# One load instead of two for the first x chunk, and the last matmul pieces shared out differently, in a fused attention + token-mixing MLP kernel

## Chip, cores, metric

The kernel runs on one core of one Trainium2 chip. The metric is the device time of one execution in microseconds (us). Most numbers come from profiled executions. "PE" is the matmul engine (TensorE), "PEld" its weight loads, DVE, ACT and POOL are VectorE, ScalarE and GpSimd, SP is the queue that issues nearly all DMAs. Times inside a profile are counted from the start of its span; the device time is about 1.8 us longer than the span. A load is "issued" while its queue is busy starting it, and "lands" when the data has arrived.

## The reference, cut to what matters

```python
xn = layernorm(A_x)                     # 2048 tokens x 1024, 16 chunks of 128 tokens
out = A_x + attention(xn) + mlp(xn)

def attention(x):   # 32 heads of 32; 4 segments of 512 tokens, causal softmax inside a segment,
    ...             # plus a linear memory carried from segment to segment; then @ wo
def mlp(x):         # mixes tokens: u = gelu(h^T w1 + b1), y = u w2 + b2, with h = layernorm(x)
    ...             # w1 is 2048 x 3584, w2 is 3584 x 2048
```

## The kernel before: the parts that matter

The first hidden layer of the MLP needs normalised x, so the kernel begins with loads of x and w1, statistics on DVE (even chunks) and ACT (odd chunks), a power on POOL, and the scaling to `h` on DVE. Ten matmuls on zeros run meanwhile ("warm-up").

```python
# start: chunk 0 in two halves of 64 rows, one on SP's queue, one on ACT's
for h, issuer in enumerate(("sp", "act")):
    fw.dma(self.xin[64 * h:64 * h + 64, 0, :], self.x_d[64 * h:64 * h + 64, 0, :],
           writes=[(self.R_xin[0], self.R_xin0)[h]], issuer=issuer)
...
for kind, c0, n in (("x", 1, 1), ("x", 2, 1), ("w", 0, 2), ("x", 3, 1), ("x", 4, 2), ...):   # all on SP
...
for _ in range(self.N_WARM):                          # N_WARM = 10
    fw.mm(self.bank(0), self.warm[:, 0:P], self.warm[:], start=True, stop=True)
...
# DVE's order: D0 = statistics of chunk 0, d2 = half the statistics of chunk 2, h0 = scale chunk 0
NORM_ORDER = (["D0 A1 S0 d2 h0 A1' A3 S1 d2' h1"] + ...)
```

In the second half of the kernel the attention of 32 units (a unit is 4 heads of one segment) is interleaved on PE with "pieces": single 128x512 matmuls of the second MLP layer and of the output projection. The pieces fill the time in which PE would wait for exponentials, masks and copies of the attention.

```python
for u in range(N_UNIT):                     # 32 units
    n0, n1, n2 = self.share(u)
    self.logits(u, 0); self.main_emit(n0)   # n0 pieces
    if u and not last_of_seg(u - 1): self.combine(u - 1)      # DVE
    self.logits(u, 1); ...; self.main_emit(n1)
    self.weigh(u, 0); self.weigh(u, 1)      # PE; DVE copies each result out of PSUM
    self.proj_q(un, 0) if un < N_UNIT else self.main_emit(8)
    self.weigh(u, 2); ...; self.weigh(u, 3)
    if un < N_UNIT: self.proj_k(un, 1)
    if last_of_seg(u): self.combine(u)
    self.main_emit(n2)                      # n2 pieces behind the last weighing
self.tail()

def share(u):
    if u < N_UNIT - 4:
        return (11, 14, 7) if u < N_GRP else (11, 15, 8)
    return (11, 16, 10) if u < N_UNIT - 2 else (11, 16, 4) if u < N_UNIT - 1 else (11, 13, 7)

def tail(self):         # output projection of the last segment, added to rows stored earlier
    ... 4 reloads of those rows ("fin") on SP ...
    product(0, 0, 7); product(1, 0, 7)      # 14 matmuls that don't need unit 31
    self.o_transpose(u, 6)                  # 4 transposes of unit 31's result, after combine(31)
    product(2, 0, 7); ...                   # the rest; each product: DVE addition, store
```

A piece of which the last matmul is done leaves PSUM by an "eviction" on DVE (`scalar_tensor_tensor` into `stg`), and the finished chunk is stored by SP.

The softmax here doesn't subtract the row's maximum and nothing guards it: scores larger than these inputs give would overflow.

Of the kernel before, what the change touches and what calls it, by code (L numbers as in the profile page):

```python
# [29 lines left out]
N_UNIT = N_SEG * N_GRP  # L30
# [315 lines left out]
class _Kernel:  # L346
# [31 lines left out]
    def alloc(self):  # L378
        nc = self.nc
        a = self.keep = _Arena(nc, self.SB_BASE, self.SB_END)  # L380
        self.ident = a.take("ident", [P, P], BF16)
        self.brow1 = a.take("brow1", [P, 32], BF16)
        self.brow2 = a.take("brow2", [P, 32], BF16)
        self.bcol = a.take("bcol", [P, 2, 32], BF16)
        self.b1c = a.take("b1c", [P, N_FCH], F32)
        self.b2c = a.take("b2c", [P, N_TCH], F32)
        self.beta_sb = a.take("beta_sb", [P, N_HEAD], BF16)
        self.gcol = a.take("gcol", [P, N_HEAD], F32)
        self.gate = a.take("gate", [P, N_GRP, 2, 4], F32)
        self.eps8 = a.take("eps8", [P, 2, 4], F32)  # L390
        self.diag = a.take("diag", [P, 4, VW], F32)
        self.ln_st = a.take("ln_st", [P, N_TCH, 12], F32)
        self.ln_mv = a.take("ln_mv", [P, N_TCH, 2], F32)
        self.ln_rs = a.take("ln_rs", [P, N_TCH, 2], F32)
        self.expo = a.take("expo", [P, N_TCH], F32)
        self.ln_sm = a.take("ln_sm", [P, N_TCH, 1], F32)
        self.vA = [a.take(f"vA{i}", [P, 4, 16, VW], BF16) for i in range(2)]
        self.MZ32 = a.take("MZ32", [P, N_GRP, GW], F32)
        self.MZbf = a.take("MZbf", [P, N_GRP, GW], BF16)
        self.srec = a.take("srec", [P, 2, 32], F32)  # L400
        self.xnT = [a.take(f"xnT{s}", [P, N_DCH, SEG_L], BF16) for s in range(N_SEG)]
        self.gT = a.take("gT", [P, N_FCH, D_MODEL], BF16)

        self.R_ident, self.R_beta, self.R_gcol, self.R_gate = Res("ident"), Res("beta"), Res("gcol"), Res("gate")
        self.R_brow1, self.R_brow2 = [[Res(f"brow{i}_{j}") for j in range(5)] for i in range(2)]
        self.R_b1c, self.R_b2c = Res("b1c"), Res("b2c")
        self.R_eps, self.R_diag = Res("eps8"), Res("diag")
        self.R_st = [Res(f"st{c}") for c in range(N_TCH)]
        self.R_rs = [Res(f"rs{c}") for c in range(N_TCH)]
        self.R_rs0, self.R_expo = Res("rs0"), Res("expo")  # L410
        self.R_vA = [[Res(f"vA{i}_{c}") for c in range(4)] for i in range(2)]
        self.R_MZ32 = [Res(f"mz32_{g}") for g in range(N_GRP)]
        self.R_MZbf = [Res(f"mzbf_{g}") for g in range(N_GRP)]
        self.R_srec = [Res(f"srec{i}") for i in range(2)]
        self.R_xnT = [Res(f"xnT{c}") for c in range(N_TCH)]
        self.R_gT = [[Res(f"gT{fc}_{h}") for h in range(2)] for fc in range(N_FCH)]
        self.R_out = [Res(f"out{c}") for c in range(N_TCH)]

        self.early_base = a.at
        e = _Arena(nc, self.early_base, self.SB_END)  # L420
        self.xin = e.take("xin", [P, N_TCH, D_MODEL], BF16)
        self.junk = e.take("junk", [P, D_MODEL], BF16)
        self.warm = e.take("warm", [P, 512], BF16)
        self.early_end = e.at = self.early_base + 40960
        self.h = e.take("h", [P, N_TCH, D_MODEL], BF16)
        w1_at = (e.at + 31) // 32 * 32
        self.w1ring = [e.take(f"w1s{i}", [P, N_TCH, 256], BF16) for i in range(3)]
        self.w1early = nc.alloc_sbuf_tensor_at("w1early", [P, N_TCH, 512], BF16, offset=w1_at)
        self.late_end = e.at
        self.R_xin = [Res(f"xin{c}") for c in range(N_TCH)]  # L430
        self.R_xin0 = Res("xin0b")
        self.R_junk, self.R_warm = Res("junk"), Res("warm")
        self.R_h = [[Res(f"h{c}_{h}") for h in range(2)] for c in range(N_TCH)]
        self.R_hh = [[self.R_h[c][h] for c in range(N_TCH)] for h in range(2)]
        self.R_w1s = [Res(f"w1s{i}") for i in range(3)]
# [78 lines left out]
    def consts(self):  # L514
        fw = self.fw
        fw.op("dve", lambda e: e.memset(self.warm[:], 0.0), writes=[self.R_warm])
        for brow, R in ((self.brow1, self.R_brow1), (self.brow2, self.R_brow2)):
            fw.op("dve", lambda e: e.memset(brow[:], 0.0), writes=[R[4]])
        self.w1_ring = _Ring(fw, [t[:] for t in self.w1ring], self.R_w1s, depth=2)
        for fp in range(N_FCH // 2):  # L520
            self.w1_ring.srcs.append(self.B_w1[:, fp * 256:(fp + 1) * 256].rearrange("(c p) f -> p c f", p=P))
        self.R_w1e = [Res(f"w1e{c}") for c in range(N_TCH)]
        for h, issuer in enumerate(("sp", "act")):
            fw.dma(self.xin[64 * h:64 * h + 64, 0, :], self.x_d[64 * h:64 * h + 64, 0, :],
                   writes=[(self.R_xin[0], self.R_xin0)[h]], issuer=issuer)
        fw.op("act", lambda e: e.activation(self.junk[:, 0:1], self.warm[:, 0:1], ACT.Gelu_apprx_tanh),
              reads=[self.R_warm], writes=[self.R_junk])
        for kind, c0, n in (("x", 1, 1), ("x", 2, 1), ("w", 0, 2), ("x", 3, 1), ("x", 4, 2), ("w", 2, 2), ("x", 6, 2),
                            ("w", 4, 4), ("x", 8, 4), ("w", 8, 4), ("x", 12, 4), ("w", 12, 4)):
            if kind == "x":  # L530
                self.load_x(c0, n)
            else:
                self.fw.dma(self.w1early[:, c0:c0 + n, :],
                            self.B_w1[c0 * P:(c0 + n) * P, 0:512].rearrange("(c p) f -> p c f", p=P),
                            writes=self.R_w1e[c0:c0 + n])
        self.w1_ring.issued = 2
        for brow, src, n, R in ((self.brow1, self.B_b1, N_FCH, self.R_brow1), (self.brow2, self.B_b2, N_TCH, self.R_brow2)):
            for j in range(4):
                fw.dma(brow[32 * j:32 * j + n, :], src.rearrange("(c q) -> c q", q=P)[:, 32 * j:32 * j + 32],
                       reads=[R[4]], writes=[R[j]])  # L540
        fw.dma(self.beta_sb[:], self.A_beta.partition_broadcast(P), writes=[self.R_beta])

        fw.op("pool", lambda e: e.memset(self.expo[:], -0.5), writes=[self.R_expo])
        fw.op("pool", lambda e: e.memset(self.ident[:], 0.0), writes=[self.R_ident])
        fw.op("pool", lambda e: e.affine_select(self.ident[:], self.ident[:], pattern=[[-1, P]],
                                                compare_op=ALU.not_equal, fill=1.0, base=0,
                                                channel_multiplier=1),
              reads=[self.R_ident], writes=[self.R_ident])
        with fw.group(reads=[self.R_warm], writes=[self.R_bank[0]]):
            for _ in range(self.N_WARM):  # L550
                fw.mm(self.bank(0), self.warm[:, 0:P], self.warm[:], start=True, stop=True)
# [65 lines left out]
    def stats_dve(self, c, halves):  # L617
        fw = self.fw
        src, st, R = self.xin[:, c, :], self.ln_st[:, c, :], self.R_st[c]
        for h in halves:  # L620
            reads = [self.R_xin[c]] + ([self.R_xin0] if c == 0 else [])
            fw.op("dve", lambda e: e.bn_stats(st[:, 6 * h:6 * h + 6], src[:, 512 * h:512 * h + 512]), reads=reads,  # L622
                  writes=[R])
        if halves[-1]:
            fw.op("dve", lambda e: e.bn_aggr(self.ln_mv[:, c, :], st.rearrange("p (a s) -> p a s", s=6)),
                  reads=[R], writes=[R])
# [390 lines left out]
    @staticmethod  # L1017
    def share(u):

        if u < N_UNIT - 4:  # L1020
            return (11, 14, 7) if u < N_GRP else (11, 15, 8)
        return (11, 16, 10) if u < N_UNIT - 2 else (11, 16, 4) if u < N_UNIT - 1 else (11, 13, 7)

    def tail(self):
        fw = self.fw
# [64 lines left out]
```

## Time and profile before

| | before |
|---|---|
| device time, 3 runs | 699.18, 700.11, 700.43 us |
| profiled span | 698.3 us |
| PE busy | 687.9 us (99%) |
| first hidden matmul | 7.20 us |
| unit 28's first logits to the four transposes | 634.06 to 684.77: 50.71 us |

The page of the profile: its first line, the busy time of each engine (us, share of the span, instructions), and the chain that ended last, by engine.

```profile
span 698.3 us, 11182 instructions
PE 687.9 (99%) x4740; PEld 327.3 (47%) x4830; DVE 260.3 (37%) x581; ACT 273.9 (39%) x301; POOL 104.8 (15%) x156
...
PE 96%; DMA 1%; issue 1%; DVE 1%; SPq 1%
```

PE is the bound. Busy time alone would not prove it, since matmul ends are modelled; the chain, 96% PE, agrees.

The beginning, from the timeline (start us, length us, engine, line, operation, out<-in, in brackets the idle time before and who ended it), with the two loads that arrive first:

```profile
0.81 1.66 SPq L216 DMA_DIRECT2D xin<-in_A_x_dram  x3
0.81 0.57 ACTq L216 DMA_DIRECT2D xin<-in_A_x_dram  x1
...
4.05 1.42 DVE L622 BATCH_NORM_STATS2 ln_st<-xin 128x6 f32<-128x512 bf16 x2 [2.80 <-DMA xin<-in_A_x_dram]
...
5.82 0.68 DVE L622 BATCH_NORM_STATS2 ln_st<-xin 128x6 f32<-128x512 bf16 x1
...
6.64 0.73 DVE L661 TENSOR_SCALAR h<-xin,ln_mv,ln_rs 128x512 bf16<-128x512 bf16 x2
...
7.20 23.08 PE L194 MATMUL ps_all<-h,w1early 128*128 128x512 bf16 x98 [1.49 <-DVE h L661]
```

Statistics of chunk 0 start when its loads are in (4.05 us), half of chunk 2's follow at 5.82, `h` at 6.64, PE at 7.20. The weight loads show PE's pace, one per matmul:

```profile
9.71 0.15 PEld L194 LDWEIGHTS ps_all<-h,w1early 128*128 128x128 bf16 x1 [0.28 <-issue]
10.04 2.04 PEld L194 LDWEIGHTS ps_all<-h,w1early 128*128 128x128 bf16 x10 [0.19 <-issue]
```

Until 10.0 us the loads are 0.427 us apart, then 0.216 (the last line merges ten). So the first 6 or 7 hidden matmuls ran at half pace, and the 128 hidden matmuls up to the next block of w1 (`w1s`) took 28.96 us (7.20 to 36.16) instead of 27.62 (128 at 0.216): 1.34 us lost.

```profile
36.16 4.05 PE L194 MATMUL ps_all<-h,w1s_81 128*128 128x512 bf16 x17
```

The end, from unit 28's first logits on:

```profile
634.06 0.63 PE L194 MATMUL ps_all<-qT_1552,kT_1555 32*128 32x256 bf16 x8
...
680.71 0.75 DVE L954 SCALAR_TENSOR_TENSOR stg_1573<-ps_all,b2c,stg_1573 128x512 bf16<-128x512 f32 x1 [1.00 <-PE ps_all L194]
...
681.33 2.97 PE L194 MATMUL ps_all<-wo_sb,xnT_70 128*128 128x512 bf16 x13
681.38 0.76 DVE L848 CAST ost_1564<-ps_all 128x264 bf16<-128x264 f32 x2
681.48 0.36 SPq L216 DMA_DIRECT2D out_dram<-stg_1573  x1
...
684.28 0.43 DVE L890 TENSOR_TENSOR o_s_1566<-prod 128x512 bf16<-128x512 bf16 x1
...
684.77 0.40 PE L200 MATMUL ps_all<-ident,o_s_1566 128*128 128x128 bf16 x4 [0.47 <-DVE o_s_1566 L890]
...
686.93 1.29 DVE L1047 TENSOR_TENSOR fin_7809<-ps_all,fin_7809 128x512 bf16<-128x512 f32 x2 [2.22 <-PE ps_all L194]
```

The 14 products behind the last weighing (681.33) end at 684.30 (13 of them have a record). The eviction (680.71) runs on DVE ahead of the two copies (681.38), then comes the combination, which ends with `o_s` at 684.71; PE stands idle for 0.47 us before the transposes.

### The profile page before, as it was taken

To read this page: it belongs to the slowest core of one execution; us is meant where nothing else is said; L and a number is where in the kernel's file an instruction comes from. 1 tells how busy PE (TensorE), PEld (TensorE's weight loads), DVE (VectorE), ACT (ScalarE), POOL (GpSimd) and SP (SyncE) were. 2 spreads that over 40 slices of the span, in tenths; PEclk is the share of its full clock that TensorE was granted. 3 is DMA by queue.
4 is the path that set the end of the run, shared out by engine and by line. 5 is a ranking of instruction groups with operands and counts; after the bars stand their busy time and mean duration, and the time that the engine had idled before them with its cause. 6 is when DMAs were issued, how large, how long until landed. Compare 5 with 4: busy or idle time off the path is not lost.

```text
span 698.3 us, 11182 instructions
## 1 busy us (share of the span) xinstructions
PE 687.9 (99%) x4740; PEld 327.3 (47%) x4830; DVE 260.3 (37%) x581; ACT 273.9 (39%) x301; POOL 104.8 (15%) x156
## 2 busy tenths in 40 slices
PE   8999999999999999999999999999999999999998
PEld 3444444444444444444444445444445444444444
DVE  6740000000012334333455545546545553444545
ACT  7531111112234445444455344455444345434440
POOL 2500000000001112211122211112211112211130
PEclk9999999999999999999999999999999999999999
DMA  8487774327036438457263634526273533445004
GB/s 307 116 194 182 167 211 119 93 60 140 1 119 134 102 72 137 102 101 139 46 137 79 129 87 93 128 52 131 63 150 79 97 95 73 113 77 121 19 21 136
DMA packets 210553, 77.17 MB, mean 111 GB/s; under 512 B 173128, under 2 KB 202824, under 8 KB 210504
## 3 DMA queue, kind: packets, MB, share of 16 engines
q1 hardware_dynamic: 210280, 76.29, 48.3%
q8 instruction: 38, 0.62, 0.4%
q10 hardware_dynamic: 224, 0.16, 0.1%
q14 instruction: 11, 0.09, 0.1%
HBM read 59.79 MB, written 5.24 MB: 93 GB/s over the span
## 4 chain that ended last, share of the span: by engine, by line
PE 96%; DMA 1%; issue 1%; DVE 1%; SPq 1%
PE ps_all L194 96%; DMA xin<-in_A_x_dram 1%; SPq L216 1%; DVE prod L886 0%; DVE stg_1573 L954 0%; DVE ost_1564 L848 0%; DVE h L661 0%; DVE o_s_1566 L890 0%; PE ps_all L200 0%; DVE srec L884 0%; DVE fin_7812 L1047 0%; DVE srec L883 0%; DVE srec L885 0%; DVE ln_mv L644 0%; DVE ln_st L622 0%
## 5 line engine op out<-in xcount | busy, mean ns | idle before, releaser
L810 ACT ACTIVATE pT<-ps_all 128x2048 bf16<-128x2048 f32 (+1 forms) x96 | 149.4, 1591 | 58.3 <-PE ps_all L194 57.2
L814 POOL TENSOR_SCALAR_AFFINE_SELECT pT<-pT 128x512 bf16<-128x512 bf16 x128 | 88.3, 703 | 554.8 <-ACT pT L810 553.7
L717 ACT ACTIVATE gT<-ps_all,b1c 128x512 bf16<-128x512 f32 x56 | 37.7, 689 | 139.3 <-PE ps_all L194 133.8
L755 DVE CAST kT_1554<-ps_all 128x512 bf16<-128x512 f32 x11 | 7.6, 690 | 170.6 <-PE ps_all L194 170.6
L194 PE MATMUL ps_all<-h,w1s_80 128*128 128x512 bf16 x251 | 55.6, 379 | 0.3
L194 PE MATMUL ps_all<-h,w1s_81 128*128 128x512 bf16 x251 | 55.6, 379 | 0.3
L194 PE MATMUL ps_all<-h,w1s_79 128*128 128x512 bf16 x250 | 55.4, 379 | 0.3
L194 PE MATMUL ps_all<-gT,w2h_897 128*128 128x512 bf16 x219 | 54.3, 380 | 0.4
L194 PE MATMUL ps_all<-gT,w2h_895 128*128 128x512 bf16 x221 | 53.7, 380 | 0.2
L194 PE MATMUL ps_all<-gT,w2h_896 128*128 128x512 bf16 x214 | 53.0, 380 | 0.6 <-issue 0.2
L194 PE MATMUL ps_all<-gT,w2h_898 128*128 128x512 bf16 x215 | 52.7, 379 | 0.5 <-issue 0.2
L848 DVE CAST ost_1563<-ps_all 128x264 bf16<-128x264 f32 (+1 forms) x64 | 23.8, 394 | 56.2 <-PE ps_all L194 56.0
L194 PEld LDWEIGHTS ps_all<-h,w1s_80 128*128 128x128 bf16 x256 | 25.0, 98 | 30.2
L194 PEld LDWEIGHTS ps_all<-h,w1s_79 128*128 128x128 bf16 x256 | 25.0, 98 | 30.2
L194 PEld LDWEIGHTS ps_all<-h,w1s_81 128*128 128x128 bf16 x256 | 25.0, 98 | 30.2
L848 DVE CAST ost_1564<-ps_all 128x264 bf16<-128x264 f32 (+1 forms) x64 | 23.7, 393 | 39.1 <-PE ps_all L194 38.9
L758 ACT ACTIVATE etmp_1568<-ps_all 128x512 bf16<-128x512 f32 x24 | 14.3, 597 | 58.8 <-DVE kT_1556 L755 20.7
L194 PEld LDWEIGHTS ps_all<-gT,w2h_898 128*128 128x128 bf16 x224 | 21.1, 98 | 25.5 <-issue 1.3
L194 PEld LDWEIGHTS ps_all<-gT,w2h_896 128*128 128x128 bf16 x224 | 20.9, 98 | 25.8 <-issue 1.7
L194 PEld LDWEIGHTS ps_all<-gT,w2h_895 128*128 128x128 bf16 x224 | 20.8, 98 | 25.2 <-issue 1.3
L194 PEld LDWEIGHTS ps_all<-gT,w2h_897 128*128 128x128 bf16 x224 | 20.7, 98 | 24.9 <-issue 1.3
L194 PE MATMUL ps_all<-wo_sb,oT_1571 128*128 128x512 bf16 x125 | 31.1, 379 | 0.2
(154 smaller groups left out, 843.7 us busy)
## 6 DMA issues: line engine op xcount, KB each, us to landing
w1s_81<-in_B_w_dram SPq DMA_DIRECT2D x4, 1024.0 KB, 5.8
w1s_79<-in_B_w_dram SPq DMA_DIRECT2D x4, 1024.0 KB, 5.6
w1s_80<-in_B_w_dram SPq DMA_DIRECT2D x4, 1024.0 KB, 5.7
wq_891<-in_A_wq_dram SPq DMA_DIRECT2D x16, 256.0 KB, 5.5
wq_892<-in_A_wq_dram SPq DMA_DIRECT2D x16, 256.0 KB, 3.5
wk_893<-in_A_wk_dram SPq DMA_DIRECT2D x16, 256.0 KB, 5.3
wk_894<-in_A_wk_dram SPq DMA_DIRECT2D x16, 256.0 KB, 3.8
w2h_895<-in_B_w_dram SPq DMA_DIRECT2D x8, 448.0 KB, 4.8
```

The lines of the kernel that those rows point to most:

```text
L194: ins = self.nc.tensor.matmul(*args, **kwargs)
L216: ins = es.eng.dma_start(out_ap, in_ap, transpose=True) if transpose else es.eng.dma_start(out_ap, in_ap)
L717: fw.op("act", lambda e: e.activation(self.gT[:, fc, half * 512:(half + 1) * 512], self.bank(b), ACT.Gelu_apprx_tanh, bias=self.b1c[:, fc: ...
L755: fw.op("dve", lambda e: e.tensor_copy(self.kT[k][:], self.bank(b)), reads=[self.R_bank[b]], writes=[self.R_kT[k]])
L758: fw.op("act", lambda e: e.activation(self.etmp[1][:], self.bank(b), ACT.Exp), reads=[self.R_bank[b]], writes=[self.R_etmp[1]])
L810: fw.op("act", lambda e: e.activation(self.pT[:, :, off:off + total], src, ACT.Exp, scale=SCALE), reads=R_src, writes=[self.R_pTu[kb] for ...
L814: fw.op("pool", lambda e: e.affine_select(d, d, pattern=[[0, 4], [1, P]], compare_op=ALU.is_ge, fill=0.0, base=0, channel_multiplier=-1), ...
L848: fw.op("dve", lambda e: e.tensor_copy(dst, self.ps[:, b, 0:n * VW]), reads=[self.R_bank[b]], writes=[self.R_ost[o][qb]])
```

## The change

Its intent: the first chunk should arrive as one load at the head of the first queue; and of the last four units' 144 pieces, six should stand behind the last weighing, so that PE has work while DVE combines unit 31.

```diff
-        for h, issuer in enumerate(("sp", "act")):
-            fw.dma(self.xin[64 * h:64 * h + 64, 0, :], self.x_d[64 * h:64 * h + 64, 0, :],
-                   writes=[(self.R_xin[0], self.R_xin0)[h]], issuer=issuer)
         fw.op("act", lambda e: e.activation(self.junk[:, 0:1], self.warm[:, 0:1], ACT.Gelu_apprx_tanh), ...)
-        for kind, c0, n in (("x", 1, 1), ("x", 2, 1), ("w", 0, 2), ("x", 3, 1), ...
+        for kind, c0, n in (("x", 0, 1), ("x", 1, 1), ("x", 2, 1), ("w", 0, 2), ("x", 3, 1), ...
 ...                        (the statistics of chunk 0 wait for one load instead of two)
-        return (11, 16, 10) if u < N_UNIT - 2 else (11, 16, 4) if u < N_UNIT - 1 else (11, 13, 7)
+        return (11, 15, 9) if u < N_UNIT - 2 else (11, 15, 2) if u < N_UNIT - 1 else (11, 13, 6)
```

With the 8 extra pieces of units 30 and 31, units 28 to 31 asked before for 37, 37, 39 and 39, but only 31 were left for the last one, so its n2 got none. After: 35, 35, 36, 38, the last 6 of them as n2.

More of the change, by code (lines that the diff above doesn't have):

```diff
@@ L430, in alloc @@
         self.R_xin = [Res(f"xin{c}") for c in range(N_TCH)]
-        self.R_xin0 = Res("xin0b")
         self.R_junk, self.R_warm = Res("junk"), Res("warm")
@@ L522, in consts @@
         self.R_w1e = [Res(f"w1e{c}") for c in range(N_TCH)]
-        for h, issuer in enumerate(("sp", "act")):
-            fw.dma(self.xin[64 * h:64 * h + 64, 0, :], self.x_d[64 * h:64 * h + 64, 0, :],
-                   writes=[(self.R_xin[0], self.R_xin0)[h]], issuer=issuer)
         fw.op("act", lambda e: e.activation(self.junk[:, 0:1], self.warm[:, 0:1], ACT.Gelu_apprx_tanh),
               reads=[self.R_warm], writes=[self.R_junk])
-        for kind, c0, n in (("x", 1, 1), ("x", 2, 1), ("w", 0, 2), ("x", 3, 1), ("x", 4, 2), ("w", 2, 2), ("x", 6, 2),
+        for kind, c0, n in (("x", 0, 1), ("x", 1, 1), ("x", 2, 1), ("w", 0, 2), ("x", 3, 1), ("x", 4, 2), ("w", 2, 2), ("x", 6, 2),
                             ("w", 4, 4), ("x", 8, 4), ("w", 8, 4), ("x", 12, 4), ("w", 12, 4)):
@@ L620, in stats_dve @@
         for h in halves:
-            reads = [self.R_xin[c]] + ([self.R_xin0] if c == 0 else [])
-            fw.op("dve", lambda e: e.bn_stats(st[:, 6 * h:6 * h + 6], src[:, 512 * h:512 * h + 512]), reads=reads,
-                  writes=[R])
+            fw.op("dve", lambda e: e.bn_stats(st[:, 6 * h:6 * h + 6], src[:, 512 * h:512 * h + 512]),
+                  reads=[self.R_xin[c]], writes=[R])
         if halves[-1]:
```

## The prediction

> What bounds it. PE: the page gives 687.9 us busy of a 698.3 us span (99%) at full clock; the chain of waits is 96% PE. From the first hidden matmul (7.20 us, timeline) PE is fed continuously, a 128x512 matmul every 0.213 us. Only its few losses can be won: before 7.20 us, the half-paced stretch behind it, 0.47 us before the last four transposes (684.77 us), and 2.3 us of output at the end. The work is the same, so at most 0.1% moves.
>
> Head. Before, x chunk 0 is two 128 KB halves on SP's and ACT's queues, both issued at 0.81 us. The DMA issues show landing after 2.6 us (SP) and 3.1 us (ACT): complete at about 3.9 us; the first statistics start at 4.05. Chunks 1 and 2 land at 4.5 and 5.45 us. The Trainium skill ("DMA: Bandwidth & Descriptors", HWDGE ordering) says the two queues are rings on the same 16 DMA engines. The trace fits: ACT's half came last, sharing the engines with chunk 1. As one load at the head of one queue it need not share. Chunks 1 and 2 are 0.95 us apart, so I estimate chunk 0 at 3.55 to 3.8 us. Then come statistics (1.42), 0.21, 0.15, POOL's power (0.55) and half of h (0.36); the next statistics need chunk 2, which just fits. The first hidden matmul moves to about 6.9 us. PE is fed from there on, so this carries to the end, except that the first 6 or 7 matmuls run 0.427 us apart until about 10.0 us; if that switch of pace stays at its time, half the gain is lost. I take -0.2 us (0 to -0.35).
>
> Tail. The last four units share 144 pieces of 0.213 us: before 37, 37, 39, 31, none behind the last weighing; after 35, 35, 36, 38, with 6 behind it. Before, 14 products (2.97 us) stand behind the last weighing, but the copies (2x0.39) and the combination on DVE (2.54) take longer, and the last piece's eviction (0.75 us, at 680.71) held up the copies. After, 20 matmuls (4.26 us) cover about 3.1 us of DVE, and the eviction stands behind the combination: -0.42. Given back: behind unit 30's last weighing 4 pieces become 2. The next logits need the copy that ended at 672.06, while PE would come at about 671.95: +0.1 to +0.2. 15 pieces instead of 16 before weighings cost nothing: unit 31 makes do with 13. Net -0.25 (0 to -0.45).
>
> Side effect: the last eviction moves behind the combination, so that chunk's store and the four reloads of partial outputs queued behind it on SP are issued about 2.5 us later (681.5 to about 684). The first reload landed 3.9 us after issue, so the first final additions start at about 688.4 instead of 686.9. They take 0.69 us against 1.7 us per product and catch up by the fifth; the last output is not touched.
>
> Time: 700.11 - 0.45, so about 699.6 us; range 698.8 to 700.4. Three runs before spread 1.25 us, more than the gain. Faster by over 2%: 0.5%; within: 99%; slower: 0.5%.
>
> Right if: first statistics near 3.7, first hidden matmul near 6.9; no idle before the four transposes, PE's last product 0.3 to 0.5 us earlier; a pause of 0.1 to 0.2 us before unit 31's logits; reloads later, additions bunched.
>
> Wrong if: one queue delivers chunk 0 no sooner; the change of pace shifts between runs by more than the gain (up to 1.4 us lost there now); the late reloads push the last additions; a removed piece uncovers an exponential or a mask.

## The result

| | before | after |
|---|---|---|
| device time, 4 runs each | 699.18, 700.43, 700.11, 698.85 | 699.98, 698.18, 700.09, 698.17 |
| median | 699.64 us | 699.08 us |
| ratio | | 0.9992, 95% interval 0.9969 to 1.0015 |
| span of the profiled run | 698.3 us | 698.2 us |
| granted clock of that run | 1.0 | 0.998 |

A ratio is the mean time of one kernel's runs over that of the other's of the same rounds, so it is not quite the ratio of the medians. The predicted 699.6 us stood against 699.08, inside the range. But the range also held the 699.64 of the kernel before, and the interval spans 1, so these times alone prove no gain, and the changed kernel's times fall into two groups 1.8 us apart. That had to be understood first. (The granted clock is the mean share of full clock that the profile records for PE; "lottery" stands below for differences between runs of one and the same kernel.) The kernel before has such a lottery too: of its 29 runs in the later sets nine had a granted clock of 0.998, all at 700.38 us or more, and the others lay between 698.58 and 700.55.

The beginning after, in the same view (the source lines have moved):

```profile
0.80 1.34 SPq L216 DMA_DIRECT2D xin<-in_A_x_dram  x3
...
3.62 1.42 DVE L617 BATCH_NORM_STATS2 ln_st<-xin 128x6 f32<-128x512 bf16 x2 [2.37 <-DMA xin<-in_A_x_dram]
...
5.87 0.69 DVE L617 BATCH_NORM_STATS2 ln_st<-xin 128x6 f32<-128x512 bf16 x1 [0.41 <-DMA xin<-in_A_x_dram]
...
6.49 0.72 DVE L656 TENSOR_SCALAR h<-xin,ln_mv,ln_rs 128x512 bf16<-128x512 bf16 x2
...
7.03 5.30 PE L194 MATMUL ps_all<-h,w1early 128*128 128x512 bf16 x16 [2.15 <-DVE h L656]
```

The statistics start 0.43 us earlier, but DVE then waits 0.41 us for chunk 2 (5.87), and PE gains 0.17 us. The pace of the weight loads:

```profile
3.79 0.59 PEld L194 LDWEIGHTS ps_all<-warm 128*128 128x128 bf16 x3 [0.28 <-issue]
7.00 0.34 PEld L194 LDWEIGHTS ps_all<-h,w1early 128*128 128x128 bf16 x3 [2.62 <-DMA w1early<-in_B_w_dram]
7.58 0.15 PEld L194 LDWEIGHTS ps_all<-h,w1early 128*128 128x128 bf16 x1 [0.24 <-issue]
...
10.57 0.15 PEld L194 LDWEIGHTS ps_all<-h,w1early 128*128 128x128 bf16 x1 [0.28 <-issue]
10.87 2.04 PEld L194 LDWEIGHTS ps_all<-h,w1early 128*128 128x128 bf16 x10 [0.15 <-issue]
```

Here PE reached full pace during the warm-up (three loads within 0.59 us from 3.79), kept it for the loads from 7.00, fell to half pace at about 7.4, and came back at about 10.8 us. The changes are about 3.4 us apart. A stretch of 3.4 us at half pace loses 1.7 us: the 128 hidden matmuls took 29.31 us (7.03 to 36.34).

```profile
36.34 3.83 PE L194 MATMUL ps_all<-h,w1s 128*128 128x512 bf16 x16
```

The profile before had lost 1.34 us in the same place, in another way: it was at half pace from the start until 10.0 us, and its granted clock was recorded as 1.0 all the same, so a recorded 1.0 does not exclude a half-paced stretch. The difference, 0.35 us, takes nearly all that this profile gained elsewhere (0.17 us at the first hidden matmul and, below, 0.26 us at the end). That is why its span is only 0.1 us shorter.

The end after:

```profile
634.25 0.63 PE L194 MATMUL ps_all<-qT,kT 32*128 32x256 bf16 x8
...
670.75 0.38 PE L194 MATMUL ps_all<-gT,w2h 128*128 128x512 bf16 x1
...
671.22 0.11 PEld L194 LDWEIGHTS ps_all<-qT,kT 32*128 32x128 bf16 x6 [0.59 <-DVE ost L843]
...
680.12 0.90 DVE L843 CAST ost<-ps_all 128x264 bf16<-128x264 f32 x2 [1.58 <-PE ps_all L194]
...
683.16 0.42 DVE L885 TENSOR_TENSOR o_s<-prod 128x512 bf16<-128x512 bf16 x1
683.50 0.74 DVE L949 SCALAR_TENSOR_TENSOR stg<-ps_all,b2c,stg 128x512 bf16<-128x512 f32 x1
684.27 0.36 SPq L216 DMA_DIRECT2D out_dram<-stg  x1
...
684.70 0.39 PE L200 MATMUL ps_all<-ident,o_s 128*128 128x128 bf16 x4
...
687.69 2.48 DVE L1042 TENSOR_TENSOR fin<-ps_all,fin 128x512 bf16<-128x512 f32 x4 [3.44 <-DMA fin<-out_dram]
...
690.73 0.69 DVE L1042 TENSOR_TENSOR fin<-ps_all,fin 128x512 bf16<-128x512 f32 x1 [0.56 <-PE ps_all L194]
```

The transposes (684.70) have no idle time before them: `o_s` (from 683.16) was long done. The eviction (683.50) now follows the combination, so the store (684.27) and the reloads come 2.8 us later than before, four additions run in one bunch from 687.69, and the fifth (690.73) waits for its product again. Moving the eviction is the smaller part of the gain: from the last matmul of unit 31's weighing to the end of `o_s` it took 3.43 us before (681.28 to 684.71) and 3.25 after (680.33 to 683.58), so about 0.18 of the 0.47 us; the six pieces cover the rest. The two were not run apart. The price is at 671.22: unit 31's first logits waited for the copy of unit 30's last weighing.

Stages give the size without the lottery at the start. From unit 28's first logits to the four transposes: 634.25 to 684.70, or 50.45 us against 50.71, a gain of 0.26. From unit 30's first logits to unit 31's: 660.95 to 671.22, or 10.27 us against 10.76. Three pieces less at 0.216 us should have given 10.11, so the pause costs 0.16 us.

### The profile page after: what moved, and what is told of

The parts are those of the page before. It is cut to its first block, busy times and chain, and to the rows that moved or that the text cites. A ratio compares the mean times of both kernels' runs of the same rounds, so it can differ in the third digit from the quotient of the medians.

```text
span 698.2 us, 11179 instructions
## 1 busy us (share of the span) xinstructions
PE 687.4 (98%) x4739; PEld 327.5 (47%) x4830; DVE 260.9 (37%) x581; ACT 274.0 (39%) x301; POOL 105.2 (15%) x156
## 4 chain that ended last, share of the span: by engine, by line
PE 96%; DMA 1%; issue 1%; SPq 1%; DVE 0%
PE ps_all L194 96%; DMA xin<-in_A_x_dram 1%; SPq L216 1%; DVE ln_st L617 0%; DVE h L656 0%; DVE ost L843 0%; DVE fin L1042 0%; PE ps_all L200 0%; DVE ln_mv L639 0%
## 5 line engine op out<-in xcount | busy, mean ns | idle before, releaser
L194 PE MATMUL ps_all<-gT,w2h 128*128 128x512 bf16 x868 | 207.4, 380 | 1.7 <-issue 0.3
L194 PE MATMUL ps_all<-h,w1s 128*128 128x512 bf16 x752 | 165.1, 379 | 0.8
L194 PEld LDWEIGHTS ps_all<-gT,w2h 128*128 128x128 bf16 x896 | 83.3, 98 | 101.2 <-issue 5.3
L194 PEld LDWEIGHTS ps_all<-h,w1s 128*128 128x128 bf16 x768 | 75.1, 98 | 90.6
L843 DVE CAST ost<-ps_all 128x264 bf16<-128x264 f32 (+1 forms) x128 | 47.6, 394 | 94.4 <-PE ps_all L194 94.0
L194 PE MATMUL ps_all<-xnT,wq 128*128 128x512 bf16 x248 | 59.8, 378 | 0.4
L194 PE MATMUL ps_all<-wv_sb,xnT 128*128 128x512 bf16 x246 | 58.1, 378 | 0.2
L194 PE MATMUL ps_all<-xnT,wk 128*128 128x512 bf16 x235 | 56.9, 379 | 1.0
L194 PEld LDWEIGHTS ps_all<-vA,pT 128*128 128x128 bf16 x1280 | 47.4, 96 | 21.7
L194 PE MATMUL ps_all<-vA,pT 128*128 128x33 bf16 x1280 | 48.2, 177 | 0.4
```

Of the source, the lines that this page charges most:

```text
L194: ins = self.nc.tensor.matmul(*args, **kwargs)
L843: fw.op("dve", lambda e: e.tensor_copy(dst, self.ps[:, b, 0:n * VW]), reads=[self.R_bank[b]], writes=[self.R_ost[o][qb]])
```

## The experiments

All kernels gave the right result.

### Each half of the change alone, and the change again

The edits: `head_only` has the new load and the old shares, `tail_only` the reverse; `after_again` is the changed kernel unchanged.

```diff
 # head_only, against the changed kernel
-        return (11, 15, 9) if u < N_UNIT - 2 else (11, 15, 2) if u < N_UNIT - 1 else (11, 13, 6)
+        return (11, 16, 10) if u < N_UNIT - 2 else (11, 16, 4) if u < N_UNIT - 1 else (11, 13, 7)
 # tail_only, against the kernel before: the same two lines the other way round
```

> Only the one-piece load of chunk 0; the pieces are shared as before. Theory A (two small independent gains, measured in the two traces as about 0.17 us in the head and 0.26 us in the tail, under a lottery of about 1.8 us in the pace of the first hidden matmuls): first statistics at 3.6 us (before 4.05), first hidden matmul at 7.0 us (before 7.20), tail as before: 50.7 us from unit 28's first logits to the four transposes, with about 0.47 us of PE idle before them. Rival B (the earlier chunk is eaten by the wait for chunk 2 and shows nowhere, all of the gain is the tail): first hidden matmul at 7.2. Time against before: A -0.2 us, B 0; both within the scatter, so the trace decides.

> Only the new shares; chunk 0 in two halves as before. Theory A: first statistics 4.05 us, first hidden matmul 7.20 us, and 50.45 us (before 50.71) from unit 28's first logits to the four transposes; unit 30 to unit 31 logits 10.27 us (10.76 before, 10.11 if the three pieces cost nothing else). Rival B: the same here. Rival C (the tail gain needs the head, for instance because the order of semaphores changed): 50.7 us. Time against before: -0.26 us, not to be told from 0 by the times alone.

> The changed kernel again, for the scatter. The Trainium skill (TensorE: Matmul & The Clock Gate, Part 1) says that the clock follows a free-running activity window of 3413 ns. Theory A: the times fall in two groups, about 698.2 us with a granted clock of 1.0 and about 700.0 us with 0.998, because in some runs PE, idle for 2.2 us before the first hidden matmul, is set back to half pace for one window (3.4 us, a loss of 1.7 us). Rival D: the two groups come from how early the loads land; then the trace shows first matmuls at times 1.8 us apart, at the same pace.

Measured, in one set: ratio to before 0.9990 (0.9977 to 1.0002) for `head_only`, 0.9995 (0.9981 to 1.0010) for `tail_only`, 0.9987 (0.9973 to 1.0002) for the change. The times decide nothing alone; the traces do. First `head_only` (PE's first hidden matmuls and the transposes), then `tail_only`:

```profile
6.86 27.79 PE L194 MATMUL ps_all<-h,w1early 128*128 128x512 bf16 x126 [1.21 <-DMA w1early<-in_B_w_dram]
...
632.39 0.63 PE L194 MATMUL ps_all<-qT,kT 32*128 32x256 bf16 x8
...
683.10 0.40 PE L200 MATMUL ps_all<-ident,o_s 128*128 128x128 bf16 x4 [0.47 <-DVE o_s L885]
```

```profile
7.48 27.79 PE L194 MATMUL ps_all<-h,w1early 128*128 128x512 bf16 x126 [1.78 <-DVE h L661]
...
633.00 0.63 PE L194 MATMUL ps_all<-qT,kT 32*128 32x256 bf16 x8
...
683.46 0.39 PE L200 MATMUL ps_all<-ident,o_s 128*128 128x128 bf16 x4
```

With the head alone the stage takes 50.71 us with 0.47 us of idle time, with the tail alone 50.46 us without it. The two halves do not depend on each other, so rival C falls. PE's first hidden matmul comes at 6.86 with one load and 7.48 with two, which speaks against B; the 7.48 is later than the expected 7.20, because DVE waited 0.56 us for chunk 2 in that run.

The changed kernel again: 697.97, 698.30, 698.31, 698.51 with a granted clock of 1.0, and 699.91, 699.95 with 0.998. The profiled run was of the lower group:

```profile
6.71 27.79 PE L194 MATMUL ps_all<-h,w1early 128*128 128x512 bf16 x126 [1.01 <-DMA w1early<-in_B_w_dram]
34.33 5.99 PE L194 MATMUL ps_all<-h,w1s 128*128 128x512 bf16 x26
```

From the first hidden matmul to the first one with the next block of w1 it took 27.62 us (128 at 0.216), against 29.31 in the first profile of the same kernel (7.03 to 36.34): 1.7 us, by pace alone, with a first matmul only 0.3 us apart. Rival D falls.

### More warm-up matmuls

```diff
-    N_WARM = 10
+    N_WARM = 16      # after_warm16 from the changed kernel, before_warm16 from the one before
```

> The changed kernel with 16 instead of 10 warm-up matmuls, so that PE idles less before the first hidden matmul. Theory A (the lottery is the set-back of PE's pace by the idle before the first hidden matmul): the 0.998 group goes; nearly all runs at 698.2 us or 0.3 us either side, mean 0.5 to 1.0 us under the changed kernel; in the trace nearly all hidden matmuls run 0.216 us apart from the first. Rival D (loads): times in two groups as before. Cost if the warm-up ends after 7.0 us: first hidden matmul later by up to 0.6 us.

Measured: 698.56 to 698.82 us over six runs, clock 1.0 in all; ratio 0.9986 (0.9973 to 0.9998). The spread fell from 2.0 us (`after_again`) to 0.26 us. The price is in the trace: the warm-up ends so late that it delays the first hidden matmul.

```profile
1.25 6.46 PE L194 MATMUL ps_all<-warm 128*128 128x512 bf16 x16 [1.25 <-DVE brow L517]
7.56 27.79 PE L194 MATMUL ps_all<-h,w1early 128*128 128x512 bf16 x126
```

The expectation held in its main point (no run near 700); its level was missed by half a microsecond, 698.7 instead of 698.2, which is about the delay from 6.9 to 7.56 us. For the same reason the mean is only 0.1 us under that of `after_again` (698.72 against 698.83), not 0.5 to 1.0: this edit bought a narrow spread and no speed.

> The kernel before with 16 warm-up matmuls, beside after_warm16 (mean 698.72 us, first hidden matmul behind the warm-up at up to 7.6 us). Theory A: the warm-up now ends after h is ready in many runs, so that most of the head's gain is hidden and nearly only the tail's 0.26 us is left: 699.0 to 699.3 us, narrow. If the head's gain does not pass through the first hidden matmul but some other way, 699.3 to 699.5 us.

Measured in a later set: 698.64, 698.77, 698.77, 699.00 and 699.44 us, mean 698.92. That is 0.2 us over `after_warm16` (698.72), which ran in another set on another chip, and just under the expected 699.0 to 699.3. It fits the reading that with the head's gain behind the warm-up nearly only the tail's is left, but 0.2 us between two sets proves nothing by itself; the profile of this run had its first hidden matmul at 7.93, still bound by chunk 2 and not by the warm-up, so the hiding was not complete.

### The change without the lottery

Thirteen warm-up matmuls end at 6.8 us even at half pace. Three changes of the changed kernel, and the kernel before, all with 13:

```diff
-    N_WARM = 10
+    N_WARM = 13
 # pause_warm13, besides:
-        return (11, 15, 9) if u < N_UNIT - 2 else (11, 15, 2) if u < N_UNIT - 1 else (11, 13, 6)
+        return (11, 15, 8) if u < N_UNIT - 2 else (11, 15, 4) if u < N_UNIT - 1 else (11, 13, 6)
 # reload_warm13, besides: the four loads of "fin" move out of tail() into reloads()
+            if u == N_UNIT - 1:
+                self.reloads()
             self.main_emit(n2)
```

> The kernel before with 13 warm-up matmuls, as the yardstick of this set: they end at 6.8 us even when all run at half pace, before h is ready (7.2 to 7.5), and cover more of the idle stretch. Theory A: most of the lottery goes, as with 16 (0.26 us spread); runs at 698.6 to 699.0 us, few or none near 700. If 13 leave too much idle, one run in three is near 700.4 with clock 0.998.

> The changed kernel with 13 warm-up matmuls, to measure the change without the lottery. Theory A: head -0.35 to -0.5 us (first hidden matmul about 6.9 instead of 7.3; h waits for chunk 2, whose landing varies by 0.4 us) plus tail -0.26: 0.6 to 0.75 us under before_warm13, 698.0 to 698.3 us. Rival B (the head gives nothing): 0.26 us under it. Rival E (the whole change is nothing but lottery): equal.

> As after_warm13, with the shares of units 28 to 31 set to 34, 34, 38, 38: 4 pieces stand again behind unit 30's last weighing, 6 behind unit 31's. Theory A: the pause of 0.16 us before unit 31's logits was the copy of the last weighing; it goes, and unit 28's first logits to the four transposes take 50.28 us (50.45 with the change, 50.71 before). If the removed pieces of units 28 and 29 uncovered something, it stays at 50.4 or more.

> As after_warm13, with the four reloads of partial outputs issued before the last pieces, so that they no longer queue behind the last eviction's store. Theory A (late reloads bunch the first four additions but are off the critical path): first addition at 686.9 us less the head's gain, directly behind its product, as before the change; the time from the four transposes to the last addition is the same 11.25 us; time equal to after_warm13 within 0.1 us. Rival F (the late reloads cost part of the tail's gain): 0.1 to 0.3 us faster.

Measured in one set, five runs each, clock 1.0 in all, none near 700:

| kernel | mean, us | lowest to highest | ratio to the kernel before (10 warm-ups) |
|---|---|---|---|
| before_warm13 | 699.07 | 698.74 to 699.43 | 0.9985 (0.9973 to 0.9998) |
| after_warm13 | 698.42 | 698.05 to 699.09 | 0.9976 (0.9964 to 0.9989) |
| pause_warm13 | 698.02 | 697.78 to 698.32 | 0.9970 (0.9958 to 0.9983) |
| reload_warm13 | 698.24 | 698.00 to 698.67 | 0.9974 (0.9961 to 0.9988) |

The change itself: 698.42 - 699.07 = -0.65 us. A second set on another chip (`after_warm13_b`, below) gave 698.42 again. With the tail's 0.26 us from the traces, 0.39 us is left for the head. The scatter of five runs makes the -0.65 uncertain by some 0.55 us (a 95% interval worked out from these runs). That leaves B in doubt by the times alone, and puts E (equal) out only narrowly; the stage times of the end, 50.70 or 50.71 us in every trace with the old shares and 50.45 or 50.46 with the changed ones, put E out clearly. The traces decide on B. PE's first hidden matmul, where it waited for `h` or w1 and not for the warm-up, came at 7.20, 7.48, 7.53 and 7.93 us in the four with a half load on each queue, mean 7.54, and at 7.03, 6.86, 6.71, 6.73, 6.97 and 7.18 in six with the one load, mean 6.91; the two sets do not overlap, though only 0.02 us lies between them. So B falls, and the head is worth about 0.4 us by the times (not clear of 0 alone), 0.6 us by the mean of the first hidden matmul. The first hidden matmuls of before_warm13 and of after_warm13:

```profile
7.53 27.84 PE L194 MATMUL ps_all<-h,w1early 128*128 128x512 bf16 x126 [1.22 <-DVE h L661]
```

```profile
6.73 27.99 PE L194 MATMUL ps_all<-h,w1early 128*128 128x512 bf16 x126 [1.14 <-DVE h L656]
```

For `pause_warm13`, unit 28's first logits and the transposes:

```profile
632.67 0.63 PE L194 MATMUL ps_all<-qT,kT 32*128 32x256 bf16 x8
...
682.95 0.39 PE L200 MATMUL ps_all<-ident,o_s 128*128 128x128 bf16 x4
```

The stage takes 50.28 us, as expected: the pause of 0.16 us is gone. The mean of `pause_warm13` is 0.40 us under after_warm13; only 0.17 of that is this stage, and the rest lies within the scatter of five runs (some 0.5 us). It has the lowest mean of all versions run: 0.30% under the kernel before in its own rounds, about half of it from the warm-up (before_warm13 has 0.15%).

For `reload_warm13`, the first additions:

```profile
684.88 1.89 DVE L1049 TENSOR_TENSOR fin<-ps_all,fin 128x512 bf16<-128x512 f32 x3 [2.60 <-PE ps_all L194]
...
693.99 0.29 DVE L1049 TENSOR_TENSOR fin<-ps_all,fin 128x128 bf16<-128x128 f32 x1 [0.15 <-PE ps_all L194]
```

The first addition now follows the transposes (682.73) by 2.15 us instead of 2.88 (682.88 to 685.76 in after_warm13). The last one follows them by 11.26 us in both (682.73 to 693.99, and 682.88 to 694.14). So the late reloads cost nothing on this path, and rival F falls by the traces. The mean of `reload_warm13` is 0.18 us under after_warm13, which taken alone would lie in F's range; the scatter of the runs is larger than that.

### Why one load is better: the issues

> The same as after_warm13, the yardstick of this set: issues on SP at 0.81, 1.26, 1.72, 2.19 us, each 0.40 to 0.43 us; first statistics 3.6 us; first hidden matmul 6.7 to 7.0 us; mean 698.2 to 698.5 us.

> As after_warm13, but chunk 0 in two halves again, both issued by SP. It parts the two differences of the head, the second issuer and the cut in two. Theory G (ACT's issue at the same time slows SP's issues: 0.57 us each instead of 0.40, in all traces with two issuers, so everything behind is issued 0.32 us later): issues take 0.40 us again, but there is one more, so chunk 1 is issued at 1.7 and chunk 2 at 2.2 us; first statistics about 3.6, first hidden matmul as in the kernel before, 7.2 to 7.5; time about 0.4 us over the yardstick. Rival H (smaller loads are issued more slowly, and that is what costs): issues of 0.5 us or more on SP.

> As after_warm13, but the whole of chunk 0 is issued by ACT, while SP begins with chunk 1. Theory G: the issues at 0.81 us take 0.57 us each, chunk 1 is issued 0.45 us earlier than in the yardstick and chunk 2 about 0.3 us earlier, but chunks 0 and 1 share the DMA engines, so chunk 0 lands at 3.8 to 4.1 us instead of 3.5; first hidden matmul 6.8 to 7.1 us, time within 0.2 us of the yardstick. Rival I (the issue is not the limit and the queues don't slow each other): chunk 0 at 3.5 us, first hidden matmul under 6.6 us.

```diff
 # halves_sp_warm13 (as after_warm13, chunk 0 in halves again, both on SP)
-        for h, issuer in enumerate(("sp", "act")):            # against the kernel before with the new shares
+        for h, issuer in enumerate(("sp", "sp")):
 # x0_act_warm13 (as after_warm13, chunk 0 whole, issued by ACT before its first activation)
+        self.load_x(0, 1)
         fw.op("act", lambda e: e.activation(self.junk[:, 0:1], ...
-        for kind, c0, n in (("x", 0, 1), ("x", 1, 1), ("x", 2, 1), ...
+        for kind, c0, n in (("x", 1, 1), ("x", 2, 1), ...
 ...                        (in load_x)
-        self.fw.dma(self.xin[:, c0:c0 + n, :], self.x_d[:, c0:c0 + n, :],
+        self.fw.dma(self.xin[:, c0:c0 + n, :], self.x_d[:, c0:c0 + n, :], issuer="sp" if c0 else "act",
```

Measured: `after_warm13_b` 698.37 to 698.54 us, mean 698.42. `x0_act_warm13` 698.96 to 699.14, mean 699.06. `halves_sp_warm13` 699.21, 699.23, 699.24 and 699.76 us, mean of the four runs 699.36; a fifth run, the profiled one, took 2505.01 us. In that run PE was busy 2499.7 of 2503.3 us, its first matmuls 0.84 us apart, a quarter of full pace, with a granted clock recorded as 1.0; it is left out of every comparison of times.

Two issuers, each with a whole 256 KB chunk (`x0_act_warm13`):

```profile
0.81 0.39 SPq L216 DMA_DIRECT2D xin<-in_A_x_dram  x1
0.81 0.41 ACTq L216 DMA_DIRECT2D xin<-in_A_x_dram  x1
...
4.67 1.42 DVE L618 BATCH_NORM_STATS2 ln_st<-xin 128x6 f32<-128x512 bf16 x2 [3.42 <-DMA xin<-in_A_x_dram]
```

Both issues at 0.81 us took 0.4 us, so an issue on ACT does not slow one on SP: theory G falls. The load of 64 rows does it, as rival H had it. In the kernel before, SP's issues took 0.57 (half of chunk 0, at 0.81), 0.56 (chunk 1, at 1.43) and 0.41 us (chunk 2, at 2.05); in the changed one 0.40, 0.42 and 0.42 (at 0.80, 1.26, 1.72). In the slow run of `halves_sp_warm13` the two halves and the load after them took 0.57, 0.57 and 0.58 us (at 0.81, 1.44 and 2.06) and the next 0.42, which agrees. So the 64-row load and the load right behind it were issued 0.16 us more slowly each, and everything later on SP came 0.32 us later (the first w1 load at 2.51 against 2.19). Why a 64-row load takes longer to issue stays open. `halves_sp_warm13` is 0.94 us slower than the yardstick, more than the 0.4 expected: with both halves on SP the second one is issued only at 1.44 us, chunk 1 at 2.06 instead of 1.26 and the first w1 load at 3.15 instead of 2.19, but since these times come from the slow run alone, how the 0.94 us is made up is not shown.

The second thing that `x0_act_warm13` shows: started at the same moment as chunk 1, chunk 0 landed 3.8 us after its issue and chunk 1 after 3.7; alone at the head of SP's queue chunk 0 took 2.6 to 2.9 us in all eight traces that have it there. It was ready at 4.6 us instead of the expected 3.8 to 4.1; the statistics start at 4.67, PE's first hidden matmul at 7.83 (7.18 in `after_warm13_b`), and the kernel is 0.64 us slower than `after_warm13_b`, where 0.2 was the most expected. The two loads that started together both arrived about 1 us later than one alone, as if they shared the engines; rival I falls too. This is what the Trainium skill ("DMA: Bandwidth & Descriptors", HWDGE ordering) says of the two queues, and this trace has the number.

## Why the prediction was right, point by point

- The bound: right. PE is 98% busy after as well, and both gains are taken off PE's stream.
- Tail, -0.42 for the idle time and +0.1 to +0.2 for the pause: right, term by term. From unit 31's first logits to the transposes 12.38 us became 13.48 with seven more pieces, which alone are worth 1.51: a gain of 0.41. The pause cost 0.16. The stage is shorter by 0.26 us against 0.25 predicted, in every fast trace with the changed kernel's shares, and not in `head_only`. (The prediction counts 0.213 us for a matmul; the traces have 0.216.)
- Side effect: right. The store moved from 681.48 to 684.27, the additions bunched and caught up by the fifth; `reload_warm13` shows that it costs nothing. The first addition came at 687.69, not 688.4.
- 15 pieces instead of 16 before the weighings cost nothing: right. Units 28 and 29 took 13.35 us each (634.25, 647.60, 660.95) against 13.78 and 13.79, which is two pieces of 0.216.
- Head: the direction and the first statistics (3.62 us, against "3.55 to 3.8" for the landing) were right, the size was short. The term was "-0.2 us (0 to -0.35)"; without the lottery it measured -0.4 by the times and -0.6 at the first hidden matmul, beyond the end of that sub-range, though the scatter (0.55 us by the times) does not exclude -0.35. Two steps of it were off. First, it held chunk 2 at its old 5.45 us, and so missed the wait that ends last in most traces with half loads. In fact chunk 2 is issued 0.33 us earlier, which the prediction did not see, because it costed the landing and not the issue of a half load. And 5.45 us was an early arrival: in the three other traces with half loads chunk 2 landed at 6.26, 6.36 and 6.76 us, and DVE waited 0.56 to 0.80 us for it. With one load it landed between 5.3 and 6.0 us, and DVE waited for it in four of eight traces (0.41 us in the changed kernel's first profile, 0.65 us in `after_warm13_b`). So both chunks bring `h` forward, and the later of the two counts, which with halves was mostly chunk 2: on the mean the first statistics start at 3.58 instead of 4.01 us, and chunk 2 lands at 5.6 instead of 6.2. Of these 0.6 us the earlier issue explains 0.33; the rest is not explained. Second, the gain is not halved by the change of pace as a rule: three of the five profiles with ten warm-up matmuls (`head_only`, `tail_only`, `after_again`) have PE at full pace from its first hidden matmul, 27.62 us for the 128, and no half-paced stretch to lose it in.
- The change of pace was named among the things that could spoil it ("shifts between runs by more than the gain"), and it did, up to 1.7 us, and made the first profile after look as if almost nothing had been won (it lost 1.69 us there, the profile before 1.34). "PE's last product 0.3 to 0.5 us earlier" was therefore wrong for that profile (0.1 us). The range of 1.6 us was right because it was made for this scatter.

The total: -0.45 predicted, -0.65 (with some 0.55 either way) measured with 13 warm-up matmuls. The -0.56 between the medians of the first four runs of each kernel is luck: it depends on how many of the four fell into the slow group.

What stays open: what decides when a run falls into the set-back. The first profile after shows one window of about 3.4 us at half pace; that the phase of such windows is free of the kernel's start is what the Trainium skill ("TensorE: Matmul & The Clock Gate", Part 1) says, and fits, but no run here controls it. Nor was it tried to let DVE scale chunk 0 before it turns to chunk 2 (`h0` ahead of `d2` in its order), which would take chunk 2 out of the way to the first hidden matmul.

## What to carry to other kernels

When a change is worth a fraction of a per cent, first find the lottery that is larger than it and switch it off (here: enough warm-up work that PE idles less before its first real matmul: 0 to 1.9 us in the traces with 13 or 16, where none of the 46 runs had a clock of 0.998, against 2.15 us in the profile with the set-back), then compare stages inside the traces. A filler piece behind a wait is worth its length only while something behind it still waits; count the pieces against the engine that must finish (here 2 pieces of 0.216 us were too few to cover a copy of 0.39 us and its hand-over, and 4 were enough; 3 were not tried). The load that everything waits for should be alone in front; splitting it over two issuers neither made it land earlier nor the issues cheaper.

## What the Trainium skill lacked or had wrong

- "TensorE: Matmul & The Clock Gate", Part 1: it says that PE goes cold after an idle window. Here a window of about 3.4 us in which PE was still busy for roughly a third (worked out from the first profile after: to 4.88 and again from 7.03 us, in a window of about 4.0 to 7.4) set it back to half pace for another 3.4 us. It also says the ramp is under 1% and should not be fitted. True (0.25%), but six more warm-up matmuls cut the spread of the times from 2.0 to 0.26 us. The page's table "Why this matters for your kernels" allows idle gaps up to about 3 us; here a gap of 2.15 us, after 3.6 us of warm-up, was followed by the set-back.
- The same page tells of the clock stuck at a quarter for over 50 us. One run here stayed there for a whole execution, 2505 us instead of 699, and the record of the granted clock said 1.0.
- "DMA: Bandwidth & Descriptors": no issue time by shape, only one figure per copy, in its part on a later chip. Here a load of 64 rows of 2 KB took 0.57 us to issue on SP, and the 128-row load right behind it 0.56 to 0.58, against 0.39 to 0.43 us for the other loads of chunks 0 to 2.
- "Trainium Kernel Development and Optimization", Key Constraints: several issuers "only saves the sequencer's issue time". Confirmed, with its price: two whole chunks issued at once landed after 3.7 and 3.8 us, one alone after 2.6 to 2.9 us.
